# Forward chunks of an adaLN transformer block: two row turns on TensorE, weight sums in every waiting unit, w2 of the last MLP product in another tile

## Chip, core and metric

One core of a Trainium2 chip runs the whole program. Its engines work side by side, each through its own instructions in order: TensorE (PE, with its weight loads PEld), VectorE (DVE), ScalarE (ACT), GpSimd (POOL) and SyncE (SP), which only starts transfers. The metric is the time of one execution in microseconds (us); lower is better. Matrix products land in PSUM, which has eight banks; everything else lies in SBUF, 128 partitions wide.

## What is computed

Output and all gradients of one transformer block over 2048 tokens, width 512, 32 heads of 16, MLP width 1792:

```python
mod = (_silu(c) @ w_mod).reshape(c.shape[0], 6, 1, -1)
sa, ca, ga, sb, cb, gb = (mod[:, i].copy() for i in range(6))
h = _layernorm(x) * (1 + ca) + sa
x = x + ga * _A_ref(h, A_wqkv, A_wo)            # 32-head softmax attention
h = _layernorm(x) * (1 + cb) + sb
x = x + gb * _B_ref(h, B_w1, B_b1, B_w2, B_b2)  # relu(h @ w1 + b1)**2 @ w2 + b2
...
_out, _vjp = jax.vjp(_f, A_x, A_wqkv, A_wo, B_w1, B_b1, B_w2, B_b2, c, w_mod)
return (_out, *_vjp(grad_out))
```

(The six parts of mod are written here as a loop; the reference writes them out.)

## The kernel before

**Three stages.** A start (prep, L856) normalises rows and makes the first keys, values and queries. The forward part then runs 512 *units* (loop at L1159): four query chunks of 512 tokens, eight head groups of four heads, sixteen key tiles of 128. After a last chunk without attention (last_chunk, L1239) comes the attention's backward pass, which is the longer half of the time and isn't touched.

**A unit.** fscore (L563) makes the scores of four heads into two of three PSUM buffers (psST) and has ScalarE take their exponentials, two instructions of 128x1024. fpv (L576) multiplies the exponentials of the unit before last with the values into oacc. After every sixteenth unit oacc is copied to ostage on VectorE, cast on GpSimd (obf) and turned by a DMA (O_un). fload (L553) fetches the next head group's keys and queries by nine small loads on GpSimd's queue, one in each unit; the ninth is the row of bounds, qt_sb<-m_st. When a unit has no other product, steady (L608) puts two idle products on TensorE, which go into oacc or, in a group's last unit, into the bank of the next paragraph.

**The dense work beside it.** As soon as a query chunk's heads are done, ffinish (L670) divides by the softmax sums (O_c) and starts a generator, dense_chunk (L321), for that chunk's output projection, layer norm, MLP, and their gradients. In each unit step (L1122) takes one step of the generator; `yield n` makes it wait n further units. Each step is about four 128x512 products into the one bank of tag pm (function mm), with VectorE emptying it. The fourth chunk is not done there but in last_chunk, after the attention. In order, a chunk does:

- turn O_c by a DMA into OT (tag T4), four output products with wo (L348), copy a_c (L349), residual with_input (L330, L331), statistics (L335, L336);
- the inverse root rsqrt_cols (L118), 16 small VectorE operations on 128x4, the normed rows xn2_c (normed, L340), turned by a DMA into h2T, scaled in place by modcol (L370); h2T is turned back to token rows h2_c by another DMA;
- 14 products with w1 (L404), rT and sT (L406, L407); 14 products with w2T (L418); gradients back through w1 (L440) and the layer norm; four products with w2 (L493) for the output; four with woT for the attention's gradient (attn_grad, L521), turned by DMAs (dOT, daT).

**Weight sums.** Every chunk adds 38 products to the weight gradients (add_chain, L225; the list is dwq): 14 for w2, 20 for w1, 4 for wo. A sum copies its product to one of four part buffers; chunk 0 stores it, later chunks add it in DRAM by an accumulating DMA on GpSimd's queue (p_st<-part). They run in units in which the generator waits. What is left when the attention ends is done in last_chunk, by fill and tick, through the tile dwbuf.

**Order of transfers.** later(lag, f) puts a call into a list that run_due empties at the right unit; sp issues on SP's queue. chunk_loads (L289) orders a chunk's loads: w1 into tile wA (lags 6 to 12), w1T into wB (20 to 26), the scaled gradient rows gf_c on GpSimd (scaled, L306, lags 14 to 17), the sums of the gradient rows on GpSimd (rowsum, L169, lags 27 to 33). Before the output product, w2 goes into wB (load_wB). Engines aren't held to the unit: a queue runs on until an instruction has to wait for data.

**PSUM.** Three score buffers of two banks each, one bank for oacc, one for tag pm: all eight.

Of the kernel before, what the change touches and what calls it, by code (L numbers as in the profile page):

```python
# [17 lines left out]
BF = dt.bfloat16  # L18
# [16 lines left out]
def kernel(  # L35
# [82 lines left out]
    def rsqrt_cols(pool, out, var, w):  # L118
        v, y, t = (pool.tile([P, w], F32, name=f"rsq{i}", tag=f"rsq{i}") for i in range(3))
        DVE.tensor_scalar(v[:], var, EPS, None, ALU.add)  # L120
        yi = y[:].bitcast(I32)
        DVE.tensor_scalar(yi, v[:].bitcast(I32), 1, None, ALU.logical_shift_right)
        DVE.tensor_scalar(yi, yi, -1, 0x5F3759DF, ALU.mult, ALU.add)
        DVE.tensor_scalar(v[:], v[:], -0.5, None, ALU.mult)
        for i in range(4):
            DVE.tensor_tensor(t[:], y[:], y[:], ALU.mult)
            DVE.tensor_tensor(t[:], t[:], v[:], ALU.mult)
            DVE.scalar_tensor_tensor(out=out if i == 3 else y[:], in0=t[:], scalar=1.5, in1=y[:], op0=ALU.add, op1=ALU.mult)
# [17 lines left out]
    with ExitStack() as ph:  # L146
# [11 lines left out]
        def mm():  # L158
            products[0] += 1
            return pools["mm"].tile([P, 512], F32, name="pm", tag="pm")  # L160

        def flat(x):
            return x.rearrange("p a b -> p (a b)")
# [15 lines left out]
        def later(lag, f, *args):  # L179
            due.append((unit[0] + lag, f, args))  # L180
# [87 lines left out]
        def next_chain():  # L268
            dwq.pop(0)[2]()

        def load_wA(src, lag):
            w = ffw.tile([P, DC, FF], BF, name="wA", tag="wA")
            for s in range(7):
                b = slice(256 * s, 256 * s + 256)
                later(lag + s, sp, w[:, :, b], src[:, :, b])
            return w

        def load_wB(src, lag, rate=1):
            w = ffw.tile([P, FC, D], BF, name="wB", tag="wB")
            for s in range(7):  # L280
                later(lag + int(s * rate), sp, w[:, 2 * s:2 * s + 2, :], src[:, 2 * s:2 * s + 2, :])
            return w
# [38 lines left out]
        def dense_chunk(c, O_c, L):  # L321
# [11 lines left out]
            def stats(ti):  # L333
                st6 = wk.tile([P, 6], F32, name="st6", tag="st6")
                DVE.bn_stats(st6[:], x1_c[:, ti, :])  # L335
                DVE.bn_aggr(mv4[:, ti, :], st6[:])  # L336
# [3 lines left out]
                DVE.tensor_scalar(xn2_c[:, ti, :], x1_c[:, ti, :], mv4[:, ti, 0:1], rstd2[:, t:t + 1], ALU.subtract, ALU.mult)  # L340

            OT = cb.tile([P, 4, DC, P], BF, name="OT", tag="T4")
            later(3, sp, OT.rearrange("p t o q -> p (t o) q"), flat(O_c), True)
            yield 6
            for ti in range(4):
                pa = mm()
                for oc in range(DC):
# [6 lines left out]
                yield 0  # L354
            with_input(3)
            stats(2)
            stats(3)
            woT = ffw.tile([P, DC, D], BF, name="woT", tag="wo")
            later(3, sp, woT[:], woT_st[:])
            h2T = cb.tile([P, 4, DC, P], BF, name="h2T", tag="T4")  # L360
            h2_c = cb.tile([P, 4, D], BF, name="h2_c", tag="h2")
            rsqrt_cols(wk, rstd2[:, ts], mv4[:, :, 1], 4)
            for ti in range(4):
                normed(ti)
            later(3, sp, h2T.rearrange("p t o q -> p (t o) q"), flat(xn2_c), True)
            yield 6
            while dwq and dwq[0][1] < c:
                yield -2
            for ic in range(DC):
                DVE.tensor_scalar(h2T[:, :, ic, :], h2T[:, :, ic, :],  # L370
                                  modcol[:, 4, ic:ic + 1], modcol[:, 3, ic:ic + 1], ALU.mult, ALU.add)
                if ic == 1:
                    yield 0

            def h2_tokens():
                while dwq and dwq[0][1] < c:
# [1 line left out]
                sp(h2_c.rearrange("p t (i d) -> p (t i) d", d=P), h2T.rearrange("p t i q -> p (t i q)"), True)  # L378

            later(4, h2_tokens)  # L380
            yield 1
            rT = cb.tile([P, FC, 512], BF, name="rT", tag="rT")
            sT = cb.tile([P, FC, 512], BF, name="sT", tag="sT")

# [44 lines left out]
                    to_tokens("dz", dzT, f0, fc + 1)  # L429
            if c == QC - 2:  # L430
                begun["w1"] = load_wA(w1_src, 1)
            yield 1
            dx1_c = cb.tile([P, 4, DC, P], BF, name="dx1_c", tag="gfT").rearrange("p t o q -> p t (o q)")
            da_c = a_c
# [42 lines left out]
            if unit[0] % TT == 0:  # L477
# [1 line left out]
            rest.pop()()  # L479
            chains = [add_chain(c, 3, FC + 4 * NS + a, D, lambda ti, a=a: O_c[:, ti, a * P:(a + 1) * P], lambda ti: da_c[:, ti, :],  # L480
                                out_3[a * P:(a + 1) * P, :]) for a in range(DC)]
            dwq[0:0] = chains
            later(9, sp, out1_v[:, ts, :], dx1_c)
            daT = cb.tile([P, 4, DC, P], BF, name="daT", tag="T4")
            later(13, sp, daT.rearrange("p t o q -> p (t o) q"), flat(da_c), True)

            w2_nat = load_wB(w2_src, 1)
            yield 6
            for ti in range(4):
                t = 4 * c + ti  # L490
                pf = mm()
# [115 lines left out]

        def steady(u):  # L608
            if 0 <= u < NF and funits[u][2] == TT - 1:
                pz = mm()  # L610
                for _ in range(2):
                    PE.matmul(pz[:], ones_bf[:], identb.unsqueeze(1).to_broadcast([P, 4, P]), start=True, stop=True)
            elif 0 <= u < NF:
                for _ in range(2):
                    PE.matmul(fcur["o"][0:DH, :], zeros[:], identb.unsqueeze(1).to_broadcast([P, 4, P]), start=False, stop=False,
                              tile_position=(0, 0), skip_group_check=True)

        def scale_heads(O_c, ou, ti, t, g):
            DVE.tensor_tensor(O_c[:, ti, 0:64 * g].rearrange("p (g h d) -> p g h d", g=g, h=4),
                              ou[:, ti, 0:g].rearrange("p g (h c) -> p g h c", h=4)[:, :, :, 0:DH],  # L620
                              r_inv[:, t, 0:4 * g].rearrange("p (g h) -> p g h", g=g).unsqueeze(3).to_broadcast([P, g, 4, DH]),
                              ALU.mult)
# [47 lines left out]
        def ffinish(qc, rr, ou, L):  # L670
            O_c = cb.tile([P, 4, D], BF, name="O_c", tag="O_c")
            pr = mm()
            for ti in range(4):
                PE.transpose(pr[:, ti * H:(ti + 1) * H], rr[0:H, ti * P:(ti + 1) * P], identf[0:H, 0:H])
            DVE.reciprocal(r_inv[:, 4 * qc:4 * qc + 4, :].rearrange("p t h -> p (t h)"), pr[:, 0:4 * H])
            for ti in range(4):
                scale_heads(O_c, ou, ti, qc * 4 + ti, HG)
            dense.append(dense_chunk(qc, O_c, L))


# [148 lines left out]
        def value_rows(t, acc):  # L829
            if t % 4 == 0:  # L830
                psp["v"] = cb.tile([P, 4, D], BF, name="vP", tag=("a_c", "xn2_c")[t // 4 % 2])
            vt = psp["v"][:, t % 4, :]
            DVE.tensor_copy(vt, acc)
            DVE.tensor_copy(vaug[:, t, 0:H, 0:DH], vt.rearrange("p (h d) -> p h d", d=DH))
            if t % 4 == 3:
                later(1, sp, v_st.rearrange("(t p) d -> p t d", p=P)[:, t - 3:t + 1, :], psp["v"][:])
# [19 lines left out]
        def prep():  # L856
# [55 lines left out]
            def widest(g):  # L912
                DVE.tensor_reduce(kmx0[:, g:g + 1], pns[g][:], AX.X, ALU.max)

            def padded_proj(acc, w, g):
                for ic in range(DC):
                    PE.matmul(acc, w[:, ic].rearrange("p h c -> p (h c)"), h1Ts[g][:, ic, :], start=(ic == 0), stop=(ic == DC - 1))
# [47 lines left out]
            value_tile(2, pv[:], False)  # L965
            pq = acc4()
            padded_proj(pq[:], wqp, 0)
            widest(3)
            DVE.tensor_reduce(kmax0, kmx0, AX.X, ALU.max)
            value_rows(2, pv[:])  # L970
            qn = cb.tile([P, 512], F32, name="qn", tag="part", bufs=4)
            ACT.activation(qn[:], pns[4][:], AF.Sqrt, scale=kmax0)
            ACT.activation(tiny0[:], onesf[:, 0:1], AF.Exp)
# [16 lines left out]
        def plan_tasks():  # L990
# [64 lines left out]
                for i in after:  # L1055
                    at(u + i, lambda: next(R["g"]))

            def b1_turn():
                pb = pools["mm"].tile([P, 2 * 512], BF, name="pb1", tag="pm")
                PE.transpose(pb[:, 0:FC], sP[0:FC, 12, 0:P], identb[0:FC, 0:FC])  # L1060
                DVE.tensor_copy(b1col[:], pb[:, 0:FC])

            def token_tile(which, g, ti):
                key = (which, g)
                if ti == 0:
# [37 lines left out]
                for ti in range(4):  # L1103
                    at(85 + 4 * g + ti, token_tile, 1, g, ti)
            query_bound(22, 0, (1,), (1, 1, 1, 2, 2, 3))
            at(21, b1_turn)
            query_bound(41, 0, (2, 3), range(1, 7))
            query_bound(50, 1, (0, 1, 2, 3), range(1, 7))
            query_bound(66, 2, (0, 1, 2, 3), range(1, 7))
# [11 lines left out]

        def step(u):  # L1122
            nonlocal wait, turn
            ripe = dwq and not open_group[0] and u >= dwq[0][0]
            if wait > 0 or not dense:
                wait = max(0, wait - 1)
                if ripe:
                    next_chain()
                return
            if ripe and turn and ((len(dwq) > 14 and fqueue) or dwq[0][3]):  # L1130
                turn = 0
                next_chain()
                return
            turn = 1
            w = next(dense[0], -1)
            if w == -2:
                next_chain()
            elif w == -1:
                dense.pop(0)
                run_due(True)  # L1140
                if not fqueue:
                    loads["L"] = chunk_loads(QC - 1)
            else:
                wait = w

        fqueue = list(range(QC - 1))
        with ExitStack() as ph2:
# [1024 lines left out]
```

## Time and profile before

| | us |
|---|---|
| median of three executions | 2465.41 (2465.1 to 2469.26) |
| profiled execution | 2467.89 |
| its span, first to last instruction | 2466.1 |
| ScalarE busy in the span | 2300.5 (93%) |
| TensorE busy, weight loads apart | 2303.2 (93%) |
| VectorE / GpSimd busy | 1826.6 / 511.5 |
| mean granted TensorE clock | 0.99 |
| first and last exponential of the forward part start | 37.1 and 990.6 |

A line of the profile names a line of the kernel, the engine, the operation, and tiles as out<-in. In a group's line, the two numbers behind the bar are all its time and the mean length of one in ns; since instructions of one engine overlap at their ends, the mean can be longer than the pitch. Then comes the idle time of the engine just before, and whose end ended it. In an order of time, a line begins with start and length in us, and what stands in brackets is the idle time before it. Three tiles in the text go by the names O_c, xn_c (xn2_c) and x_c (x1_c), as the profile cuts digits off. The four GpSimd products of one chunk (L306) and an undisturbed and a disturbed row of L330 can be told apart only by time, not in the groups.

### The profile page before, as it was taken

The numbers are of one execution on the slowest core, as the hardware profiler recorded it, in microseconds if no ns is written. First come the engines' busy times: TensorE is split into PE (matmuls) and PEld (weight loads), VectorE is DVE, ScalarE is ACT, GpSimd is POOL, SyncE is SP. The second block draws the span as 40 slices with busy tenths as digits, with TensorE's granted clock in tenths as the row PEclk, the third lists the DMA queues.
The fourth block names the chain that finished last, engine by engine and source line by source line (L and its number), as shares of the span: only waits on it lengthen the run. The fifth ranks groups of instructions, "written<-read, shape, count | busy, mean of one in ns | idle before, by whom it ended". The sixth has DMA issues, their size and how long they took to land. (4 is left out here: it accounts for less than half of the span.)

```text
span 2466.1 us, 49726 instructions
## 1 busy us (share of the span) xinstructions
PE 2303.2 (93%) x18870; PEld 766.2 (31%) x18870; DVE 1826.6 (74%) x2361; ACT 2300.5 (93%) x3581; POOL 511.5 (21%) x692
## 2 busy tenths in 40 slices
PE   8898889988988999999999999999999999999999
PEld 3232223222322322442333232333233233222244
DVE  6555163455435554578999999999999999999985
ACT  8999999999999999628999999999999999999965
POOL 2111132423544353201110101101011010110112
PEclk9999999999999999999999999999999999999999
DMA  4478474357657875979999999999999999999997
GB/s 156 122 171 179 144 158 107 91 165 154 96 86 165 161 121 126 258 229 173 206 195 203 202 207 204 203 202 207 203 213 202 202 208 207 204 206 204 205 230 176
DMA packets 1217027, 440.81 MB, mean 179 GB/s; under 512 B 1093750, under 2 KB 1189620, under 8 KB 1216532
## 3 DMA queue, kind: packets, MB, share of 16 engines
q1 hardware_dynamic: 1171604, 381.60, 81.5%
q0 software_dynamic: 23472, 33.77, 8.1%
q10 hardware_dynamic: 21712, 22.27, 3.7%
q8 instruction: 148, 2.42, 0.4%
q14 instruction: 91, 0.75, 0.1%
HBM read 94.63 MB, written 70.78 MB: 67 GB/s over the span
## 5 line engine op out<-in xcount | busy, mean ns | idle before, releaser
L1650 DVE TENSOR_TENSOR dS_u<-psD_u,E_u 128x1024 bf16<-128x1024 f32 x1024 | 1185.7, 1216 | 66.7 <-PE psD_u L1648 23.4
L574 ACT ACTIVATE ET<-psST 128x1024 bf16<-128x1024 f32 x1024 | 942.5, 1275 | 12.1 <-PE psST L572 11.6
L1634 ACT ACTIVATE E_u<-psS_A 128x512 bf16<-128x512 f32 x768 | 511.2, 666 | 10.4 <-DMA d_st<-dltT 7.8
L1634 ACT ACTIVATE E_u<-psS_B 128x512 bf16<-128x512 f32 x768 | 504.3, 657 | 9.7 <-PE psD_u L1648 5.2
L1648 PE MATMUL psD_u<-iv,ido 32*128 32x512 bf16 x2048 | 408.5, 386 | 0.4
L572 PE MATMUL psST<-qt_sb,kt_sb 32*128 32x512 bf16 x2048 | 314.3, 384 | 53.9 <-ACT ET L574 45.9
L1634 ACT ACTIVATE E_u<-psS_C 128x512 bf16<-128x512 f32 x512 | 334.6, 653 | 2.5 <-PE psS_B L1628 1.0
L1628 PE MATMUL psS_A<-ik,iq 32*128 32x512 bf16 x768 | 292.1, 380 | 11.4 <-ACT E_u L1634 1.0
L1628 PE MATMUL psS_B<-ik,iq 32*128 32x512 bf16 x768 | 294.0, 383 | 8.2 <-ACT E_u L1634 0.6
L1735 POOL TENSOR_TENSOR dQacc<-dQacc,dqtmp 128x512 f32<-128x512 f32 x64 | 81.3, 1270 | 846.6 <-ACT dqtmp L1730 785.5
L1628 PEld LDWEIGHTS <-iq 32*128 32x128 bf16 x2048 | 130.2, 91 | 314.8 <-issue 298.8
L1690 PE MATMUL accVK<-dS_u,qz 128*32 128x512 bf16 x2048 | 212.3, 388 | 0.5 <-PE psD_u L1648 0.2
L588 PE MATMUL oacc<-ET,vaug 128*32 128x512 bf16 x2048 | 207.2, 392 | 0.0
L1699 PE MATMUL accVK<-E_u,dOs_tok 128*16 128x512 bf16 x2048 | 202.0, 384 | 0.0
L1628 PE MATMUL psS_C<-ik,iq 32*128 32x512 bf16 x512 | 193.8, 379 | 4.3 <-ACT dqtmp L1730 0.2
L572 PEld LDWEIGHTS <-kt_sb 32*128 32x128 bf16 x2048 | 84.3, 91 | 338.9 <-issue 322.9
L1717 PE MATMUL dqacc<-dsT,KS_tok 128*32 128x512 bf16 x2048 | 146.1, 383 | 21.4 <-DMA dsT<-dS_u 7.5
L250 DVE COPY part<-pm 128x512 f32<-128x512 f32 (+2 forms) x103 | 63.5, 616 | 121.1 <-PE pm L232 118.6
L1794 ACT ACTIVATE dsT<-ptT 128x1024 bf16<-128x1024 bf16 x126 | 144.2, 1144 | 3.2 <-PE ptT L1680 3.0
L1648 PEld LDWEIGHTS <-ido 32*128 32x128 bf16 x2048 | 105.4, 91 | 99.2 <-issue 93.6
L1690 PEld LDWEIGHTS <-qz 128*32 128x32 bf16 x2048 | 58.5, 94 | 177.1 <-issue 161.9
L1735 POOL TENSOR_TENSOR dQst<-dQacc,dqtmp 128x512 bf16<-128x512 f32 x32 | 40.6, 1270 | 265.7 <-ACT dqtmp L1730 265.7
(433 smaller groups left out, 2683.9 us busy)
## 6 DMA issues: line engine op xcount, KB each, us to landing
p_st<-part POOLq DMA_DIRECT2D x36, 256.0 KB, 5.4
kt_sb<-qkT_st POOLq DMA_DIRECT2D x124, 64.0 KB, 3.5
wA<-in_B_w_dram SPq DMA_DIRECT2D x28, 256.0 KB, 6.4
wB<-w1T_st SPq DMA_DIRECT2D x21, 256.0 KB, 3.6
wA<-w2T_st SPq DMA_DIRECT2D x21, 256.0 KB, 5.5
wB<-in_B_w_dram SPq DMA_DIRECT2D x21, 256.0 KB, 4.0
p_st<-part POOLq DMA_DIRECT2D x25, 192.0 KB, 4.6
p_st<-part SPq DMA_DIRECT2D x18, 256.0 KB, 2.4
```

Of the source, the lines that this page charges most:

```text
L572: PE.matmul(ps[:, hi, :], kt_sb[r:r + 32, kt * P:(kt + 1) * P], qt_sb[r:r + 32, :], start=True, stop=True, tile_position=(r, 0))
L574: ACT.activation(ET[:, 2 * pair:2 * pair + 2, :], ps[:], AF.Exp, scale=SCALE)
L588: PE.matmul(oacc[32 * hq:32 * hq + 32, :], lhsT, ET[:, hq, :], start=(kt == 0), stop=(kt == TT - 1), tile_position=(0, 32 * hq), skip_grou ...
L1628: PE.matmul(psS[:], st["q"][r:r + 32, qt * P:(qt + 1) * P], st["k"][r:r + 32, kc * 512:kc * 512 + 512], start=True, stop=True, tile_positi ...
L1634: ACT.activation(bst[u][0][:, hq, :], sst.pop((u, hq))[:], AF.Exp, scale=SCALE)
L1648: PE.matmul(psD[:, hi, :], st["do"][r:r + 32, qt * P:(qt + 1) * P], st["v"][r:r + 32, kc * 512:kc * 512 + 512], start=True, stop=True, til ...
L1650: DVE.tensor_tensor(dS_u[:, 2 * pair:2 * pair + 2, :], psD[:], E_u[:, 2 * pair:2 * pair + 2, :], ALU.mult)
L1690: PE.matmul(cur["vk"][32 * hq:32 * hq + 32, :], hst[hg]["qz"][:, qt, hq, :], bst[u][1][:, hq, :], start=(qt == 0), stop=False, tile_positi ...
L1699: PE.matmul(acc[32 * hq:32 * hq + DH, :], dOs_tok[:, qt, (hg * 4 + hq) * DH:(hg * 4 + hq + 1) * DH], E_u[:, hq, :], start=False, stop=(qt ...
L1717: PE.matmul(acc[32 * hq:32 * hq + 32, :], KS_tok[:, kc * 4 + kt, h * DH:h * DH + 32], tT[:, :, hq * 4 + kt, :], start=(kt == 0), stop=(kt ...
L1735: POOL.tensor_tensor(dst2, dst, tmp[:], ALU.add)
L1794: ACT.activation(dst, pt[:], AF.Identity)
```

## The change

The attention output and the normed rows are turned by TensorE transposes into the pm bank, two tiles of 128 tokens at a time, and VectorE copies (or scales) them out; both DMAs and most of the waiting around them go. Three short waits are put in instead. Weight sums also run in steps of the generator that make no product, and the wo sums go behind three others. When the last forward chunk is done, sums run only while more than ten are left. In chunks 0 and 1, w2 goes into tile wA, loaded from the start of the first gradient product on, every third unit. steady leaves out the pair in a group's last unit while there is any dense work, weight sum or planned task. In the finish of a chunk (ffinish) the generator's first step is put off by one unit. The turn of b1 goes from unit 21 into the start (prep).

```diff
             OT = cb.tile([P, 4, DC, P], BF, name="OT", tag="T4")
-            later(3, sp, OT.rearrange("p t o q -> p (t o) q"), flat(O_c), True)
-            yield 6
+
+            def turned(src, half):
+                pt = pools["mm"].tile([P, 2, DC, P], BF, name="ptc", tag="pm")
+                products[0] += 1
+                for k in range(2):
+                    for oc in range(DC):
+                        PE.transpose(pt[:, k, oc, :], src[:, 2 * half + k, oc * P:(oc + 1) * P], identb[:])
+                return pt
+
+            for half in range(2):
+                pt = turned(O_c, half)
+                DVE.tensor_copy(OT[:, 2 * half:2 * half + 2], pt[:])
+                yield 0
             for ti in range(4):
                 pa = mm()
...
             with_input(3)
             stats(2)
+            yield 1
             stats(3)
...
             rsqrt_cols(wk, rstd2[:, ts], mv4[:, :, 1], 4)
+            yield 1
             for ti in range(4):
                 normed(ti)
-            later(3, sp, h2T.rearrange("p t o q -> p (t o) q"), flat(xn2_c), True)
-            yield 6
+                if ti == 1:
+                    yield 0
             while dwq and dwq[0][1] < c:
                 yield -2
-            for ic in range(DC):
-                DVE.tensor_scalar(h2T[:, :, ic, :], h2T[:, :, ic, :],
-                                  modcol[:, 4, ic:ic + 1], modcol[:, 3, ic:ic + 1], ALU.mult, ALU.add)
-                if ic == 1:
-                    yield 0
+            for half in range(2):
+                pt = turned(xn2_c, half)
+                for ic in range(DC):
+                    DVE.tensor_scalar(h2T[:, 2 * half:2 * half + 2, ic, :], pt[:, :, ic, :],
+                                      modcol[:, 4, ic:ic + 1], modcol[:, 3, ic:ic + 1], ALU.mult, ALU.add)
+                yield 0
...
             later(4, h2_tokens)
-            yield 1
...
             if c == QC - 2:
                 begun["w1"] = load_wA(w1_src, 1)
+            else:
+                w2_nat = ffw.tile([P, FC, D], BF, name="w2_nat", tag="wA")
+                for s in range(7):
+                    later(1 + 3 * s, sp, w2_nat[:, 2 * s:2 * s + 2, :], w2_src[:, 2 * s:2 * s + 2, :])
...
-            dwq[0:0] = chains
+            dwq[3:3] = chains
...
-            w2_nat = load_wB(w2_src, 1)
-            yield 6
+            if c == QC - 2:
+                w2_nat = load_wB(w2_src, 1)
+                yield 6
+            else:
+                yield 3
...
         def steady(u):
             if 0 <= u < NF and funits[u][2] == TT - 1:
+                if dense or dwq or plan:
+                    return
                 pz = mm()
...
                 scale_heads(O_c, ou, ti, qc * 4 + ti, HG)
+            nonlocal wait
+            wait = 1
             dense.append(dense_chunk(qc, O_c, L))
...
             padded_proj(pq[:], wqp, 0)
+            pb = psp["p"].tile([P, 2 * 512], BF, name="pb1", tag="pk", bufs=3)
+            PE.transpose(pb[:, 0:FC], sP[0:FC, 12, 0:P], identb[0:FC, 0:FC])
             widest(3)
             DVE.tensor_reduce(kmax0, kmx0, AX.X, ALU.max)
             value_rows(2, pv[:])
+            DVE.tensor_copy(b1col[:], pb[:, 0:FC])
...
-            at(21, b1_turn)
...
         def step(u):
             nonlocal wait, turn
-            ripe = dwq and not open_group[0] and u >= dwq[0][0]
+            ripe = dwq and not open_group[0] and u >= dwq[0][0] and (dense or fqueue or len(dwq) > 10)
...
             turn = 1
+            count = products[0]
             w = next(dense[0], -1)
...
             else:
                 wait = w
+                if ripe and products[0] == count and not open_group[0]:
+                    next_chain()
```

More of the change, by code (lines that the diff above doesn't have):

```diff
@@ L1056, in query_bound @@
                     at(u + i, lambda: next(R["g"]))
[L1058 to L1061, printed above, removed]
             def token_tile(which, g, ti):
```

## The prediction

> **What bounds the kernel now.** I read the page first, then a table of busy time in stretches of 25 us, then who waited for whom, then the order of time around one chunk. The page's own chain of waits is of no use here: its lines add up to a few per cent and lie at the very end, far from the change. The stretches tell the stages apart (columns: PE, PEld, DVE, ACT, POOL busy, granted clock, DMA share, GB/s).
>
> ```profile
> span 2466.1 us, 49726 instructions
> L574 ACT ACTIVATE ET<-psST 128x1024 bf16<-128x1024 f32 x1024 | 942.5, 1275 | 12.1 <-PE psST L572 11.6
> ```
> ```profile
> 525.00:550.00 25.00, 21.68 (x158) 7.11 (x157) 13.28 (x18) 25.00 (x29) 7.28 (x11) 1.00 0.83 223
> ...
> 575.00:600.00 25.00, 22.20 (x159) 7.53 (x156) 16.33 (x23) 24.27 (x27) 8.69 (x13) 1.00 0.72 144
> ...
> 700.00:725.00 25.00, 19.91 (x127) 5.91 (x126) 5.79 (x8) 19.78 (x23) 6.75 (x10) 0.90 0.87 115
> ...
> 1050.00:1075.00 25.00, 25.00 (x157) 13.31 (x156) 16.92 (x43) 9.36 (x13) 1.85 (x9) 1.00 0.90 268
> ```
>
> From 37 to 992 us ScalarE sets the pace: 1024 exponentials in 942.5 us are 0.92 us each, 1.84 us for a unit of two, and it stood idle only 12.1 us before them. All the work of the change in that stretch is free unless it makes an exponential late, and it can win at most those 12.1 us. From 994 to 1118 us (the last chunk) TensorE is the bound: 25.00 of 25. After that nothing is changed.
>
> TensorE works strictly in program order: scores of unit u, attention values of u-2, then that unit's product. So a product that waits for VectorE holds up the next scores. How much waiting is free? Three score buffers: just after the scores of u, ScalarE still has three exponentials, 2.76 us, to do.
>
> **The change part by part.** I count units by the yields. In chunk 1 the finish is at unit 264, and the third output product, row 543.7 (the fourth starts at 545.55), is unit 274, so unit u's product starts at 545.55 + 1.84 (u - 275). Before: output products 272 to 275, root 276, first MLP product 286. After: turns 266 and 267, output products 268 to 271, root 274, normed rows 276 and 277, turns 277 and 278, first MLP product 279. The other chunks lie 128 units away, at the same phase.
>
> *Attention output turned on TensorE.* Eight transposes take 0.72 us (row of ptx, 128x128, x8), the copy 0.75 us (0.56 us for 128x768, by columns 4/3). The rows it needs are scaled by 528.2 and the first turn is due at 529.0: 0, bounds 0 and 0.5 us a chunk. The two DMA turns that leave SP's queue lay under units without a product: 0.
>
> *Normed rows turned on TensorE.* This is the place. These rows of before are in the order of time (start, length):
>
> ```profile
> 545.17 1.17 POOL L306 TENSOR_TENSOR gf_c<-g_c,modbc 128x512 bf16<-128x512 bf16 x1
> ...
> 545.27 3.23 DVE L330 TENSOR_TENSOR atmp<-a_c,modbc 128x512 bf16<-128x512 bf16 x1
> 548.54 1.42 DVE L331 TENSOR_TENSOR x_c<-atmp,x_c 128x512 bf16<-128x512 bf16 x1
> ...
> 551.27 0.41 DVE L330 TENSOR_TENSOR atmp<-a_c,modbc 128x512 bf16<-128x512 bf16 x1
> ...
> 558.15 0.16 DVE L128 SCALAR_TENSOR_TENSOR rstd<-rsq,rsq 128x4 f32<-128x4 f32 x1
> 558.35 1.38 DVE L340 TENSOR_SCALAR xn_c<-x_c,mv,rstd 128x512 bf16<-128x512 bf16 x4
> 564.14 1.38 DVE L370 TENSOR_SCALAR h2T<-h2T,modcol 128x512 bf16<-128x512 bf16 x4 [4.41 <-DMA h2T<-xn_c]
> ```
>
> VectorE took 3.23 and 1.42 us for what takes 0.41 undisturbed, because GpSimd was scaling grad_out rows (four products of 1.17 us, 1.65 us apart). Before, nobody waits for that: ten units without a product follow, VectorE has 4.41 us to spare for the DMA turn. After, TensorE waits for exactly this chain. Working it out for chunk 1 with the pitches of these rows (copy 0.58, residual 0.79, statistics 0.82): VectorE is through the third statistics at 543.5 and copies the accumulator (0.65) to 544.15. That releases GpSimd: cast 0.6, four row loads 1.9, so its four products run from 546.65 to 552.8. VectorE: last statistics to 545.0, root 2.95 us to 548.1, two normed rows to 548.9. The transposes are due at 549.2, so there is 0.3 us of room, and the second half of the root, eight two-input operations, and all four normed rows fall into GpSimd's products.
>
> Bounds: (a) nothing blocked: then only the two halves cost. Each half keeps the one product bank for 0.72 us of transposes, four column scalings of 0.41 us from PSUM (row of L1306) and some 0.25 us of signalling, 2.6 us in place of 1.84, and the first MLP product waits for the last; two such steps eat the lead, loss 0.5 us. (b) Only 128x512 rows blocked, as such rows of the trace are (a scaling of that form, L463: 0.93 instead of 0.41): normed rows at 549.7 and 551.5, scores two units later 1.15 us late and the next 0.75, loss 1.9 us. (c) The 128x4 operations too: two or three of them get through between two products, the second normed row is done at about 552.4, TensorE stands 3.2 us, ScalarE loses 2.35 + 1.4 + 0.85 = 4.6 us. No row shows a 128x4 two-input operation meeting such a product. I take 3.5 us, nearer to (c), since among 128x512 operations with two SBUF inputs every one that began inside such a product waited. Three chunks: +10.5, between 1.5 and 13.8.
>
> The Trainium skill, "SBUF — State Buffer", section "SBUF: two separate sides", says that a VectorE operation with two SBUF inputs and a GpSimd operation that reads SBUF lock one port pair for a whole instruction and the loser blocks fully. By that rule (c) holds and the time would be 2476. The 1.42 us agrees; 3.23 us is two products, more than the rule gives.
>
> *The MLP's first loop* (14 units, 1.87 us each and three or four at 2.1 where GpSimd's sums meet L407) overdraws by some 1.3 to 2 us. Before, the full lead absorbed most and 0.73 us was lost (25.00 - 24.27); after, the lead is gone: +0.5 us a chunk, +1.5, between 0 and 3.6.
>
> *The bias turn, moved into the start.* It adds a copy of 0.17 us in front of the first queries: +0.1. At unit 21, where it was, 1.8 us are lost between 75 and 100 us in a stretch of low clock; I count 0 there, bounds -1.8 and 0.
>
> *Weight sums.* 38 a chunk. By the yields the last forward chunk ends at unit 496 instead of 504, sums run down to ten, four more follow at the end, and 6 instead of 11 are left for the last chunk. The 11 stand in the trace (7 and 4):
>
> ```profile
> p_st<-dwbuf POOLq DMA_DIRECT2D x7, 192.0 KB, 10.4
> p_st<-dwbuf POOLq DMA_DIRECT2D x4, 128.0 KB, 5.5
> ```
>
> Six fill the wait for the layer norm either way. The other five run in the TensorE-bound loop: 1.28 us for the one after 1012 us, four at 0.43: -3.0, bounds -3.0 and -1. No sums in the last units before the end: -0.9 (TensorE waited 0.72 us there on a sum's copy, and ScalarE 0.94), bounds -1.1 and 0.
>
> *The filler left out* at the end of a head group: 0.59 us of TensorE where it waits 0.37 us for ScalarE anyway: 0.
>
> *w2 in the other tile.* The seven 256 KB loads of chunks 0 and 1 move ahead of out_dram<-dx_c and the daT turn on SP's queue, three units apart, due by unit 342 for a product at 348: 0 by themselves. They matter for the one large stall of before:
>
> ```profile
> 699.08 12.60 SPq L177 DMA_TRANSPOSE daT<-a_c  x1
> ...
> 705.57 0.54 POOL L551 DMA_DIRECT2D qt_sb<-m_st  x1
> ...
> 721.15 0.62 PE L572 MATMUL psST<-qt_sb,kt_sb 32*128 32x512 bf16 x4 [4.65 <-DMA qt_sb<-m_st]
> ```
>
> The m row of the next queries took 15.4 us to land (median 3.2), behind four accumulating sums, the w2 loads and the daT turn; TensorE stood 4.65 us, the clock fell to 0.51, ScalarE lost 5.22 + 0.84 = 6.1 us. After, chunk 1 has no burst of w2 loads there, but five sums in a row (343 to 347) with the daT turn and an m row due at 346; chunk 2 has seven sums in a row (467 to 473) over the seven w2 loads and the daT turn, and an m row at 474. I take half the stall back: -3, bounds -6.1 (none left) and +6 (once in each chunk).
>
> **Sum**, against the profiled execution's own 2467.9 us (its span 2466.1 and 1.8 around it; 2.5 above the median of the three runs, 2465.4): 2467.9 + 10.5 + 1.5 + 0.1 - 3.0 - 0.9 - 3.0 = **2473 us**.
>
> **Rivals.** *B, faster.* GpSimd's products do not meet the root, or the lead covers it: case (a), no stall of the m row, half of the loss at unit 21 gone: 2467.9 + 1.5 + 0.1 - 3.0 - 0.9 - 6.1 - 0.9 = 2459. For it: 0.3 us of room undisturbed, and the m row is late once in 31 loads. Against it: the products start 2.5 us after the accumulator's copy whatever the shift, and VectorE needs 4.75 us. It decides as soon as a chunk loses under 1 us at its turns. *D, next to nothing.* Case (b): 5.7 and 1.5 in place of 10.5 and 1.5: 2468. *C, much slower.* The accumulating sums in a row take the DMA engines from the m row in chunks 1 and 2: 2473 + 3 + 6 = 2482. For it: the same mixture as at 699 us, one sum longer or more; against it: chunk 2 of before has sums, w2 and daT close together and loses nothing. *That it does not do what it says:* the rule of ten holds sums back, so six are left over, not none; that is in every case above.
>
> The Trainium skill, "TensorE: Matmul & The Clock Gate", section "What's actually happening", halves the clock after an idle window of about 3.4 us. The 4.65 us wait agrees. The 3.2 us of case (c) lie just under it. If each chunk's wait passed it, what ScalarE lost after that wait (6.1 less the first 4.24) would come three times on top, an estimate of 2478.
>
> **Chances.** Forecast 0.43 (own range 2469 to 2478), B 0.25, D 0.17, C 0.15. A measurement of this kernel tells 0.2%, 4.9 us, from no change: faster is below 2460.5, slower above 2470.3. Faster 0.20 (most of B); within 0.26 (the rest of B, most of D, the forecast's lower end); slower 0.54. The range 2457 to 2483 leaves out the ends of B and C, some 0.18.
>
> **What would show it.** Right: TensorE's ptc transposes from normed rows waiting 2 to 4 us on VectorE in each of three chunks, root operations of 128x4 of a microsecond, more than 20 us of idle before L574, six p_st<-dwbuf. Wrong: idle before L574 under 10 us (B), or waits of TensorE on m_st (C). The forecast falls if GpSimd's products come earlier or later than the root, or if small two-input operations pass them.

## The result, and the profile after

The changed kernel took 2509.0 us (median of four, 2500.11 to 2514.34) beside 2465.26 us: a ratio of 1.0173, with an interval of 1.0146 to 1.02. That is 44 us slower, where 2473 us, 7.6 us above the median before, had been forecast; the range ended at 2483. The direction was right, the size was not.

First the page's group of exponentials of the changed kernel, with its span (behind the bars: busy time and mean length; idle time before them and its cause):

```profile
span 2507.3 us, 49811 instructions
...
L594 ACT ACTIVATE ET<-psST 128x1024 bf16<-128x1024 f32 x1024 | 946.5, 1257 | 44.2 <-PE psST L592 43.8
```

ScalarE now stands idle 44.2 us before its exponentials, nearly always for scores, where it stood 12.1. The stretches of 25 us say where (changed kernel; columns as before: PE, PEld, DVE, ACT, POOL, granted clock, DMA share, GB/s):

```profile
300.00:325.00 25.00, 17.56 (x116) 5.40 (x114) 20.51 (x48) 18.61 (x21) 9.75 (x14) 0.74 0.20 51
...
425.00:450.00 25.00, 20.89 (x142) 6.77 (x140) 15.55 (x32) 22.55 (x25) 16.11 (x19) 0.97 0.29 72
...
550.00:575.00 25.00, 16.99 (x108) 5.45 (x106) 19.54 (x46) 18.62 (x21) 9.58 (x14) 0.80 0.19 51
...
675.00:700.00 25.00, 20.87 (x136) 6.68 (x136) 15.67 (x32) 22.05 (x25) 18.36 (x22) 0.95 0.34 68
...
800.00:825.00 25.00, 18.75 (x116) 5.77 (x117) 20.63 (x48) 19.32 (x22) 9.54 (x14) 0.73 0.27 51
...
925.00:950.00 25.00, 20.98 (x140) 6.62 (x137) 14.85 (x30) 22.02 (x24) 18.07 (x20) 0.93 0.48 121
950.00:975.00 25.00, 19.56 (x126) 5.77 (x122) 6.48 (x9) 19.91 (x22) 7.85 (x12) 0.93 0.77 88
```

There are two series with a place in every chunk: one at 300, 550 and 800 us (ScalarE 18.6 to 19.3 of 25, clock 0.73 to 0.80), where the normed rows are turned, and one at 425, 675 and 925 us (ScalarE 22.0 to 22.6), where the last gradient of the chunk's MLP is finished; and a last hole at 950, in the third chunk alone. The first series was the forecast's. Here is its first place in the order of time (start, length; in brackets the idle time before):

```profile
309.96 3.41 DVE L126 TENSOR_TENSOR rsq<-rsq 128x4 f32<-128x4 f32 x1
310.18 1.16 POOL L306 TENSOR_TENSOR gf_c<-g_c,modbc 128x512 bf16<-128x512 bf16 x1
...
311.84 1.17 POOL L306 TENSOR_TENSOR gf_c<-g_c,modbc 128x512 bf16<-128x512 bf16 x1
...
313.41 1.27 DVE L127 TENSOR_TENSOR rsq<-rsq,rsq 128x4 f32<-128x4 f32 x1
...
314.72 0.16 DVE L128 SCALAR_TENSOR_TENSOR rsq<-rsq,rsq 128x4 f32<-128x4 f32 x1
...
315.31 1.02 DVE L128 SCALAR_TENSOR_TENSOR rstd<-rsq,rsq 128x4 f32<-128x4 f32 x1
...
316.84 1.03 PE L349 MATMUL ptc<-identb,xn_c 128*128 128x128 bf16 x8 [4.30 <-DVE xn_c L340]
...
318.51 1.94 ACT L594 ACTIVATE ET<-psST 128x1024 bf16<-128x1024 f32 x2 [4.27 <-PE psST L592]
...
324.43 1.94 ACT L594 ACTIVATE ET<-psST 128x1024 bf16<-128x1024 f32 x2 [1.48 <-PE psST L592]
```

An operation on four values per partition took VectorE 3.41 us, through two GpSimd products, and three operations of the root were held up in all (3.41, 1.27 and 1.02 us). TensorE waited 4.30 us for the normed rows (4.64 and 3.39 us in the other chunks), and because its clock was then halved (1.03 us for the eight transposes, which take 0.62 in e1 below), ScalarE lost more in the units behind. The second series the forecast did not have:

```profile
442.06 0.82 PE L232 MATMUL pm<-tk,h_c 128*128 128x384 bf16 x4
...
443.60 1.26 DVE L484 TENSOR_TENSOR uqb<-dxn,tqb 128x512 bf16<-128x512 bf16 x1
...
446.21 0.42 DVE L489 TENSOR_TENSOR a_c<-dx_c,modbc 128x512 bf16<-128x512 bf16 x1
...
446.55 0.55 DVE L250 COPY part<-pm 128x384 f32<-128x384 f32 x1
447.13 8.26 SPq L177 DMA_DIRECT2D p_st<-part  x5
447.15 0.81 PE L232 MATMUL pm<-tk,h_c 128*128 128x384 bf16 x4 [3.19 <-DVE part L250]
...
448.39 1.94 ACT L594 ACTIVATE ET<-psST 128x1024 bf16<-128x1024 f32 x2 [2.45 <-PE psST L592]
```

A weight sum runs in the unit of the last gradient's VectorE chain; its product was done at 442.9, but its copy stands behind that chain and comes at 446.55. Until then the one product bank is taken, and the next sum waits 3.19 us, with the scores behind it. And in the third chunk only, two copies wait for a free part buffer, that is for an accumulating transfer, while a daT turn is under way:

```profile
942.51 13.00 SPq L177 DMA_TRANSPOSE daT<-a_c  x1
...
950.62 0.69 DVE L250 COPY part<-pm 128x512 f32<-128x512 f32 x1 [2.09 <-DMA p_st<-part]
...
955.39 0.69 DVE L250 COPY part<-pm 128x512 f32<-128x512 f32 x1 [4.08 <-DMA p_st<-part]
956.13 1.02 PE L513 MATMUL pm<-wB,sT 128*128 128x512 bf16 x4 [3.09 <-DVE part L250]
```

### The profile page after: what moved, and what is told of

It reads as the page before. It is cut to its first block, busy times and chain, and to the rows that moved or that the text cites. A ratio compares the mean times of both kernels' runs of the same rounds, so it can differ in the third digit from the quotient of the medians.

```text
span 2507.3 us, 49811 instructions
## 1 busy us (share of the span) xinstructions
PE 2313.7 (92%) x18920; PEld 768.2 (31%) x18920; DVE 1837.0 (73%) x2384; ACT 2304.4 (92%) x3576; POOL 509.0 (20%) x692
## 5 line engine op out<-in xcount | busy, mean ns | idle before, releaser
L594 ACT ACTIVATE ET<-psST 128x1024 bf16<-128x1024 f32 x1024 | 946.5, 1257 | 44.2 <-PE psST L592 43.8
L592 PE MATMUL psST<-qt_sb,kt_sb 32*128 32x512 bf16 x2048 | 302.4, 392 | 45.1 <-ACT ET L594 42.4
L592 PEld LDWEIGHTS <-kt_sb 32*128 32x128 bf16 x2048 | 78.5, 91 | 319.1 <-issue 305.4
L1741 PE MATMUL dqacc<-dsT,KS_tok 128*32 128x512 bf16 x2048 | 147.7, 387 | 17.8 <-DMA dsT<-dS_u 5.1
```

Of the source, the lines that this page charges most:

```text
L592: PE.matmul(ps[:, hi, :], kt_sb[r:r + 32, kt * P:(kt + 1) * P], qt_sb[r:r + 32, :], start=True, stop=True, tile_position=(r, 0))
L594: ACT.activation(ET[:, 2 * pair:2 * pair + 2, :], ps[:], AF.Exp, scale=SCALE)
L1741: PE.matmul(acc[32 * hq:32 * hq + 32, :], KS_tok[:, kc * 4 + kt, h * DH:h * DH + 32], tT[:, :, hq * 4 + kt, :], start=(kt == 0), stop=(kt ...
```

## The experiments

Times are medians beside the kernel before on the same chip (2464.8 to 2466.7 us in each set). Executions of one kernel differ by 10 us and more, so single waits and the length of the forward part (first exponential's start to last one's end) tell more than the medians.

**e1, the scaling out of the way.**

```diff
-                later(14 + ti, scaled, ti)
+                later(2 + ti, scaled, ti)
```

> The changed kernel with GpSimd's four products gf_c<-g_c,modbc twelve units earlier (lag 2 to 5 in place of 14 to 17), so that they are done before the output products; nothing else. Theory (GpSimd's products block VectorE's two-input operations of the root): the rsq operations take 0.16 us each, TensorE's waits before ptc<-xn_c of 4.30, 4.64 and 3.39 us fall under 1 us, the three turn stretches lose 1 to 2 us instead of 8.2, 8.2 and 7.3, and the time is 2509 - 19 = 2490 us (2484 to 2497). Rival (the chain of VectorE is too long for the three yields, whoever runs beside it): waits of 2 us and more stay, 2500 to 2509 us.

Measured: 2485.32 us, ratio 1.0079 (1.0048 to 1.0111). The same root in its trace:

```profile
311.06 0.16 DVE L126 TENSOR_TENSOR rsq<-rsq 128x4 f32<-128x4 f32 x1
...
313.58 0.62 PE L349 MATMUL ptc<-identb,xn_c 128*128 128x128 bf16 x8
...
317.84 1.02 PE L417 MATMUL pm<-h2T,wA 128*128 128x512 bf16 x4 [0.80 <-DVE h2T L385]
```

No wait of TensorE is left before the turn, and only 0.80 us for the column scalings behind it. The forward part is 971.4 us in place of 990.7. The rival falls: the same yields suffice once GpSimd is out of the way. The three turn stretches lose 1.6, 0.8 and 0.9 us beside e9, the second profile of before.

**e2, no sums in steps without a product.**

```diff
-            count = products[0]
...
                 wait = w
-                if ripe and products[0] == count and not open_group[0]:
-                    next_chain()
```

> The changed kernel without the weight sums in steps of the generator that make no product. Theory (such a sum, put right behind a long VectorE chain, holds the one product bank until its copy gets its turn): TensorE's waits on a sum's copy after the last gradient product (3.19, 3.20, 2.87 us) and after the last attention gradient (1.36, 1.36 us) vanish, ScalarE gains 3.5 + 3.5 + 3.0 + 2.0, the time is 2509 - 12 = 2497 us (2492 to 2501). Rival (the sums only run a unit later and meet the same chain): the waits stay at 2 us and more, 2504 to 2511 us.

Measured: 2497.95 us, 1.0124 (1.0089 to 1.016); forward part 979.8 us. In chunks 0 and 1 the waits on a sum's copy behind the last gradient product are gone, and those behind the last attention gradient too. In the third chunk 1.63 us of it stay and two waits for part buffers, 2.85 and 3.29 us, remain.

**e3, both edits.**

> Both edits of the two runs before at once. Theory (two causes independent of each other, which make up most of the loss): 2509 - 19 - 12 = 2478 us (2470 to 2485), and ScalarE's idle time before the exponentials falls from 44.2 to about 14 us. Rival (most of the 44 us lies elsewhere, in the clock or in the transfers): above 2490 us.

Measured: 2483.68 us, 1.0065 (1.004 to 1.009); 23.0 us idle before the exponentials, forward part 967.6 us. The time lies in the theory's range, but not for its reason alone: 14 us of idle time had been expected. The two causes add in the first two chunks, and the third chunk's wait took part of the gain back. In the order of time of e3:

```profile
916.05 5.99 SPq L177 DMA_TRANSPOSE daT<-a_c  x1
...
931.52 0.69 DVE L250 COPY part<-pm 128x512 f32<-128x512 f32 x1 [10.64 <-DMA p_st<-part]
932.27 1.86 PE L232 MATMUL pm<-a_c,O_c 128*128 128x512 bf16 x4 [9.65 <-DVE part L250]
```

**e4, the turns alone on the kernel before:** both turns on TensorE as in the change, with their short waits and the put-off first step, and nothing else of it.

```diff
-            later(3, sp, OT.rearrange("p t o q -> p (t o) q"), flat(O_c), True)
-            yield 6
+            for half in range(2):
+                pt = turned(O_c, half)
+                DVE.tensor_copy(OT[:, 2 * half:2 * half + 2], pt[:])
+                yield 0
...
-            later(3, sp, h2T.rearrange("p t o q -> p (t o) q"), flat(xn2_c), True)
-            yield 6
+                if ti == 1:
+                    yield 0
...
+            for half in range(2):
+                pt = turned(xn2_c, half)
```

> The kernel before with the two turns on TensorE, their short waits and the put-off first step alone: weight sums, w2 tile, filler and bias turn as before. Theory (the turns alone cost about 8 us a chunk): 2465 + 19 to 24 = 2487 us (2481 to 2491), with TensorE waiting 3.4 us and more before ptc<-xn_c in three chunks. Rival (the price that was forecast, 3.5 us a chunk and 1.5 more): 2477 us.

Measured: 2504.46 us (2485.48 to 2505.88), 1.013 (1.0077 to 1.0184). TensorE's waits before the turns, from three stretches of its order of time:

```profile
320.05 1.03 PE L349 MATMUL ptc<-identb,xn_c 128*128 128x128 bf16 x8 [3.16 <-DVE xn_c L340]
```
```profile
562.58 1.03 PE L349 MATMUL ptc<-identb,xn_c 128*128 128x128 bf16 x8 [4.61 <-DVE xn_c L340]
```
```profile
808.36 1.03 PE L349 MATMUL ptc<-identb,xn_c 128*128 128x128 bf16 x8 [4.63 <-DVE xn_c L340]
```

The forward part was 978.1 us, 29 us longer than the second profile of before (e9). The three turn stretches hold 7.4, 6.7 and 6.7 us of that, so the turns alone bring 20.8 us, about half of what the changed kernel's forward part loses. More than expected came from elsewhere: some 5.5 us at 953 us, where the third chunk's scores were late, and a backward part of 1372.0 us (see the end). The scores waited for their row of bounds, ordered at 939.05 us beside the daT turn and four accumulating sums, which took 14.0 us to land.

**e5, no turns:** the kernel of e2 with both turns by DMA and the old waits, so e4's diff taken back:

```diff
-                pt = turned(O_c, half)
...
+            later(3, sp, OT.rearrange("p t o q -> p (t o) q"), flat(O_c), True)
+            yield 6
...
-                pt = turned(xn2_c, half)
...
+            later(3, sp, h2T.rearrange("p t o q -> p (t o) q"), flat(xn2_c), True)
+            yield 6
```

> The changed kernel with both turns done by DMA as before (and the waits as before), and without the sums in steps that make no product; w2 in the other tile, the order of the wo sums, the rule of ten, the filler left out and the bias turn as changed. Theory (what is left of the change saves about 2 us at the filler, 2 at the end of attention and 2 in the last chunk, and only the third chunk's wait for part buffers can cost): 2462 us (2455 to 2470), no wait of TensorE over 1.5 us in the first two chunks. Rival (the new order of sums and of w2 costs by itself, turns or not): 2475 us and more.

Measured: 2467.8 us, 1.0013 (0.9999 to 1.0028), forward part 950.2 us, no wait of 0.75 us in chunks 0 and 1; in the third chunk one of 2.65 us at its finish, on a sum's copy, and one of 1.37 us at its last gradient. The rest of the change costs next to nothing, and wins nothing that can be told.

**e6, w2 back in wB** (on e3, one burst in all chunks).

```diff
-                w2_nat = ffw.tile([P, FC, D], BF, name="w2_nat", tag="wA")
...
-            if c == QC - 2:
-                w2_nat = load_wB(w2_src, 1)
-                yield 6
-            else:
-                yield 3
+            w2_nat = load_wB(w2_src, 1)
+            yield 6
```

> The kernel of e3_both (early scaling, no sums in steps without a product) with w2 loaded in one burst into tile wB in all three chunks, as before. Theory (the burst of w2 takes the DMA engines from the accumulating sums and the row loads; in e3_both only the third chunk has such a burst, and TensorE waits 9.65 us there): in the second chunk, between 690 and 740 us, a wait of 2 us or more on a part buffer or a row of bounds appears, which e3_both has not, and the time is 3 to 10 us above that of e3_both: 2490 us (2485 to 2496). Rival (the tile of w2 changes nothing): no wait over 1 us there, 2478 to 2486 us.

Measured: 2478.85 us, 1.0057 (1.0035 to 1.008). No wait of 1 us or more between 690 and 740 us: this theory fell. One profile can't rule the place of w2 out, though, since such waits differ between executions (see e9). In the third chunk 9 us were lost again.

**e7, no sums while w2 loads in the third chunk** (on e3).

```diff
+                held[0] = True
                 yield 6
+                held[0] = False
```

`ripe` is false while it is set.

> The kernel of e3_both with no weight sums in the six units of the third chunk in which w2 is loaded. Theory (four part buffers full of accumulating transfers that the burst holds up): the wait of 9.65 us goes, the first forward part gets 10 us shorter (957 to 959 us in place of 967.6), the few sums more in the last chunk cost 1 to 3 us, and the time is 8 us under that of e3_both: 2475 us (2468 to 2479). Rival (the DMA engines are full whoever asks, and the next transfer in line is late instead): a wait of 4 us or more at 900 to 945 us under another name, 2480 to 2486 us.

Measured: 2478.49 us, 1.0053 (1.0034 to 1.0073). The wait is gone and the forward part is 954.9 us, but the last chunk takes 121.1 in place of 116.9 us; eight sums are left to it in place of six. So the sums must be there for the wait; what holds them up, e11 and e12 ask.

**e8, the small parts alone on the kernel before** (no filler, the rule of ten).

```diff
+                if dense or dwq or plan:
+                    return
...
-            ripe = dwq and not open_group[0] and u >= dwq[0][0]
+            ripe = dwq and not open_group[0] and u >= dwq[0][0] and (dense or fqueue or len(dwq) > 10)
```

> The kernel before with two parts of the change alone: the filler left out in a group's last unit, and sums after the last forward chunk only while more than ten are left. Theory (three losses of before at 160, 190 and 219 us, 0.92 + 0.69 + 0.69 us, come from the filler's copy-bound product bank, and 1.9 us at the end of attention from sums): the forward part gets 3 to 4 us shorter, the last chunk no longer: 2461 us (2457 to 2465). Rival (the filler costs nothing, as was forecast): 2463 to 2466 us.

Measured: 2466.62 us, 1.0004 (0.9988 to 1.0019). The three losses at the filler are gone (from unit 128 on its exponentials are 1.0 to 1.3 us ahead of those of e9), but those at the end of attention are all still there; forward part 947.5 us. The rule of ten held no sum back in this kernel: eleven p_st<-dwbuf are left for the last chunk, as before. Nothing that the median shows.

**e9 and e10, both kernels once more.**

> The kernel before once more, for a second profile. Theory (the 4.65 us wait for a row of bounds at 721 us and the length of the unchanged backward part are matters of the single execution): the wait is not at 721 us again, or of another size, so that the forward part is 948 to 955 us long; the backward part is 1346 us + 0.36 x its time at half clock, as in nine profiles so far (1355.5 to 1372.0 us with 28 to 70 us), and longer than the first profile's 1355.5. Rival (the wait belongs to the kernel's order): 954.6 us again with a wait of 4 us and more at 721 us.

> The changed kernel once more, for a second profile. Theory: the waits of TensorE before ptc<-xn_c (over 3 us, three times), behind the last gradient product (about 3 us, three times) and on the third chunk's part buffers (3 us and more) are there again, the forward part is 988 to 993 us long; the backward part differs from 1363.1 us by as much as its time at half clock says. Rival (part of the 36 us was the single execution's): a forward part under 985 us.

Measured: 2465.72 and 2506.11 us. The page's group for the kernel before, then for the changed one:

```profile
L574 ACT ACTIVATE ET<-psST 128x1024 bf16<-128x1024 f32 x1024 | 942.4, 1283 | 6.4 <-PE psST L572 5.5
```
```profile
L594 ACT ACTIVATE ET<-psST 128x1024 bf16<-128x1024 f32 x1024 | 946.5, 1255 | 44.8 <-PE psST L592 44.2
```

The stall at 721 us of the first profile of before does not come again: its forward part is 948.8 us, not 954.6, and its backward part 1359.8 us with 44.4 us at half clock (1362.0 by the expectation's line). The changed kernel repeats itself: 991.3 us beside 990.7, with waits of 3.76, 4.47 and 4.45 us at the turns and 3.20, 3.20 and 2.87 behind the gradients.

**e11 and e12, what holds up the third chunk's sums** (both on e3): first the order of the daT turn, then the row loads.

```diff
-            later(13, sp, daT.rearrange("p t o q -> p (t o) q"), flat(da_c), True)
+            later(18 if c == QC - 2 else 13, sp, daT.rearrange("p t o q -> p (t o) q"), flat(da_c), True)
```
```diff
-                later(i // (2 if qc == 0 else 1), row_load, to, fro)
+                later(i // (2 if qc in (0, QC - 1) else 1), row_load, to, fro)
```

> The kernel of e3_both with the DMA turn daT<-a_c of the third chunk ordered five units later, behind the copies rrows<-ostage, where it stands in e5_no_turns and before. Two theories for the 9.65 us wait on a part buffer in e3_both. A (the turn runs beside the accumulating sums and holds them up): the sums' waits on part buffers of 4 us and more go, the forward part is 957 to 961 us in place of 967.6, 2476 us (2470 to 2480). B (the sums alternate with the row loads on GpSimd's queue, as they do not in e5_no_turns, and that is what makes them late): a wait of 4 us and more stays, 2480 to 2487 us.

> The kernel of e3_both with the nine row loads of the fourth query chunk's head groups issued in pairs in five units in place of one in each of nine, so that most of the third chunk's sums come behind them. A (the daT turn is what holds the sums up): a wait of 4 us and more on a part buffer stays, 2479 to 2487 us. B (the row loads between the sums): it falls under 2 us, the forward part is 957 to 961 us, 2476 us (2470 to 2480).

Measured: 2477.74 us, 1.0049 (1.003 to 1.0069), and 2480.99 us, 1.007 (1.0042 to 1.0098). TensorE's longest wait there, with the daT turn at 942 us (e11), and with the row loads moved but the turn at 916.94 (e12):

```profile
923.89 1.02 PE L232 MATMUL pm<-a_c,O_c 128*128 128x512 bf16 x4 [2.12 <-DVE part L250]
```
```profile
931.32 1.87 PE L232 MATMUL pm<-a_c,O_c 128*128 128x512 bf16 x4 [7.83 <-DVE part L250]
```

The forward parts are 958.1 and 964.9 us. Theory A holds in the main: with the turn behind the sums, the wait shrinks from 9.65 to 2.12 us; with the rows moved, most of it stays. A single wait is a weak sign, though: e6, with the third chunk of e3, has none over 1.75 us there and loses time all the same. By units 470 to 480, beside e9, e3, e12 and e6 with the turn at the sums lose 13.5, 11.7 and 8.2 us, e11 3.9 us, and e7 without the sums nothing. So the turn explains most of it; what the rest in e11 comes from is open. In e5 the same turn is issued at 935.94 us, behind the copies of the softmax sums on SP's queue and after the last sum. What the turns on TensorE changed is the phase: the third chunk's end comes some eight units earlier, where nothing on SP's queue holds the turn back until the sums are done.

No version tried is faster than the kernel before.

## Why the prediction missed its range

Against the second profile of before, whose forward part has no stall, the changed kernel's profile is 42.6 us longer: forward part +41.9, last chunk 116.6 for 118.8, backward part 1363.1 for 1359.8, and 0.4 earlier at the start. Where the forward part lost, read from when each exponential starts in the one trace and in the other:

| stretch (units) | forecast | measured |
|---|---|---|
| turns and the MLP's first products (128-160, 272-288, 392-416) | +12 | 8.1 + 7.9 + 6.5 = +22.5 |
| w2T late for the second MLP product, small waits (160-216, 288-344, 416-464) | 0 | +1.8 |
| sums behind a VectorE chain (216-272, 344-376) | 0 | 4.8 + 5.0 = +9.8 |
| third chunk: the same, and part buffers (376-392, 464-480) | 0 | 1.5 + 9.1 = +10.6 |
| filler left out (to 128) | 0 | -1.2 |
| end of attention (480 on) | -0.9 | -1.9 |
| late row of bounds (in one execution) | -3.0 | 0 |

**The turns: the right mechanism, half the size.** That GpSimd's four products would start some 2.5 us before the turns and meet the root held (2.4 us at the first place), and case (c), priced at 4.6 us a chunk, came out as a mechanism; e1 shows that it is they, for without them the three stretches lose 3.2 us (4.7 to 7.1 us in the five other kernels with the same edit, and 1.8 us in e5 without the turns). The step that failed is the 3.5 us taken for a chunk, and its upper bound of 4.6 with it. Two things were mis-sized. In (c) two or three operations got through between two products and TensorE stood 3.2 us; one operation waited for two products in a row, as the 3.23 us row of before had shown for 128x512 rows, all normed rows came after the last product (in the first place at 316.37 us, when the product had ended at 316.30), and TensorE stood 3.39 to 4.64 us. And what follows the wait was not charged: the halved clock stretched the first MLP product to 1.87 us, and ScalarE lost another 0.56, 1.48 and 0.28 us in the units behind the first of the three waits. By the Trainium skill, "SBUF — State Buffer", section "SBUF: two separate sides", whoever starts first keeps the shared ports for the whole instruction; the trace agrees that VectorE's operation ends only after a whole product, and adds that it can lose the next round too (3.41 us). It doesn't show that the first to start wins: by the recorded starts, VectorE's operation began 0.22, 0.38 and 0.35 us ahead of the first product in the three chunks, and takes 0.16 us elsewhere. Why it lost that round is open. The forecast's estimate of 2478 with the clock rule was nearer than the sum, and still short by 31 us.

**Weight sums: the step that left out a cost.** The forecast said that sums also run in steps without a product and priced only what they save. It did not ask where the copy of such a sum stands in VectorE's order. It stands behind the whole chain of the gradient in the same step, holds the product bank, and costs about 4 us a chunk there; e2 shows it for the first two chunks (4.1 and 4.0 us at units 216 to 232 and 344 to 352 become 0.9 and 0.1). Behind the last attention gradient e2 takes the 1.36 us waits away too, but the exponentials gain 0.6 us there in chunk 0 (units 232 to 256) and nothing in chunk 1 (352 to 376). That this would take the gain of five fewer sums several times over was in none of the rivals.

**Rival C: half right, in the wrong transfer.** It had the accumulating sums in a row colliding with the transfers around daT, at 6 us in each of two chunks. It came in the third chunk only, and the sums were the late ones, not the row of bounds: their four buffers stayed full. e7 and e11 show both partners, the sums and the turn. In e4 it was the row of bounds, as the rival had it.

**Late row of bounds: a gain that was not there.** Half of the 6.1 us stall of the profiled execution was booked as saved. The second profile has no such stall, though the same transfers run beside the turn at 699 us at the same times: there the sums issued with it land after 7.6 to 7.7 us and the row of bounds after 6.1, where they took 13.4 to 17.3 and 15.4 us in the first (8.9 for the row in e8). So the meeting belongs to the kernel's order, and its price to the execution. The change took the sums away from the turn in chunk 1 and brought them to it in the third chunk.

**What held.** The filler's removal is free (it even wins 1.2 us; in e10 a loss of 1.4 us before unit 40 hides that); six p_st<-dwbuf are left for the last chunk, which got 2.2 us shorter (forecast 3.0); the bias turn costs nothing that shows; more than 20 us of idle time before the exponentials was named as the sign of the forecast, and is there.

None of the cases had a weight sum that holds the one product bank behind a chain on VectorE.

## What to carry to other kernels

Before a DMA turn is replaced by one on TensorE, write out who else is on VectorE and GpSimd in exactly those units: a wait that was cover for ten units becomes cover for none. For each product added to a single-buffered bank, find the place of its copy in VectorE's order; if a chain stands before it, the bank is busy for that chain. And take a second profile of the kernel before, before a stall in the first one is booked as a gain.

## What was not expected of the hardware

**Half clock without a long wait.** In the changed kernel TensorE's clock halved at 291.5 us although no wait in the 7 us before it was over 0.53 us; TensorE was 78% and 74% busy in the two stretches of 3.4 us before it. In the unchanged backward part it halved for one such stretch behind stretches in which TensorE was 96 to 98% busy: in the changed kernel at 1475.9 and 1496.4 us, and at 1827.5, 1848.0 and 1868.4 us, some 20.5 us apart. (Busy time here counts a product of 32 of the 128 rows or columns, as most of that part's are, like a full one; whether that bears on the clock no run asks.) Three stretches of that part (columns as above):

```profile
1472.60:1475.90 3.30, 3.18 (x27) 0.91 (x24) 3.02 (x4) 3.30 (x8) 0.11 (x1) 1.00 1.16 215
1475.90:1479.30 3.40, 3.40 (x20) 1.08 (x20) 2.89 (x3) 2.96 (x5) 0.00 (x0) 0.50 1.23 229
1479.30:1482.70 3.40, 3.20 (x37) 1.24 (x39) 2.39 (x3) 2.82 (x5) 0.00 (x0) 1.00 1.39 170
```

The Trainium skill, "TensorE: Matmul & The Clock Gate", section "What's actually happening", puts the halving down to an idle window of about 3.4 us; the waits of 4.30 and 4.64 us agree, these stretches do not. Over the fourteen profiles of this study the backward part, the same code in all, took 1353.0 to 1372.0 us and grew by about 0.34 us with each us at half clock (17.8 to 68.3 us, added up from each trace's record of the clock; correlation 0.88). That may be much of what executions of one kernel differ by; it is not shown, since only two kernels have a second profile. Whether the change itself adds to it stays open: both profiles of the changed kernel had more half clock there (51.8 and 48.5 us) than both of before (27.3 and 44.4), but so had e5 without its turns (49.2), and e3 and e12 with them had 27.3 and 17.8.

**A turn against accumulating stores.** In e3, the four accumulating stores issued within 6 us of the DMA turn of 128x2048, from 915.9 us on, took 14.0 to 15.5 us to land, where the median of such stores in the changed kernel's page is 5.3 and 5.4. In e11, with the same loads of w2 just before but without the turn, the four stores took 6.5 to 7.1 us. In e5, with no load of w2 in the 20 us before, the turn of the second chunk met three stores that took 9.7 to 10.7 us, where the two ahead of them took 3.4 and 3.8. Not every meeting is dear: a single store issued 0.3 us ahead of that turn took 4.0 us in e3, and in e9 the three behind it took 7.6 to 7.7, hardly more than in e11. What in the transfers decides, no run here asks.
